# Moving Softplus behind the visit's Square and cutting the Erfs of the second group in two halves

## The chip, the cores and the metric

The kernel runs on one core of one Trainium2 chip (trn2). The metric is the device time of one execution in microseconds (us). A core has five engines that work side by side, each through its own list of instructions in order: TensorE (PE in the profile, with its weight loads as PEld), VectorE (DVE), ScalarE (ACT), GpSimd (POOL) and SyncE (SP), which starts the DMA transfers.

## What is computed

An attention block without softmax, its output normalised by its root mean square, and behind it a feed-forward block with the gate h * erf(softplus(h)).

```python
# q, k, v: (8, 8, 576, 64)   g_norm: (64,)
kv = np.einsum('bhsd,bhse->bhde', k, v)
out = np.einsum('bhsd,bhde->bhse', q, kv)
rms = np.sqrt(np.mean(out * out, axis=-1, keepdims=True) + 1e-06)
x = out / rms * g_norm                 # then (B, H, S, D) -> (B*S, H*D) = (4608, 512)
# w_in: (512, 2048)   w_out: (2048, 512)
h = x @ w_in
sp = np.maximum(h, 0.0) + np.log1p(np.exp(-np.abs(h)))
g = h * erf(sp)
y = g @ w_out                          # (4608, 512)
```

## The kernel before

**Groups and units.** The 4608 rows are worked on in nine groups of 512 rows. A group T < 8 holds the first 512 rows of one batch element; the ninth holds the last 64 rows of all eight. The hidden width 2048 is cut into FC = 16 units of 128, and BATCH = 4 units make a period. For one unit, TensorE makes a 128 x 512 block of h; ScalarE and VectorE bring it to SBUF and gate it; TensorE multiplies it with w_out.

**Two stages.** In the first stage (the loop over n from L848, groups T = 0 and 1, here called group 1 and group 2) the weights are also converted and cut. Group 1 uses plain fp32 products (L900). Group 2 multiplies with cut forms: every product (`product`, L651) makes two partial results, n_ps with 8 matmuls and m_ps with 4 (L659). ScalarE copies n_ps to h with a scale (L915), VectorE adds m_ps (L637), ScalarE takes the Softplus (L928), and after each fourth unit the Erfs (L935); VectorE multiplies h by the result (`gates`, L846) LAG - 1 = 4 units later, and one unit after that the plain projection with w_out runs (L715). In group 2 ScalarE also starts the cut of weights for the later groups (`w_upper`, L621), which VectorE finishes (L624, L627) and the SP queue stores to DRAM.

In the second stage (the loop over m from L1001, groups T = 2 to 8) both products use cut forms that are loaded back from DRAM (`load_parts`, L799). A period has four hidden products, each with a copy of n_ps (L1050), an add of m_ps (L637) and a Softplus (L1065); then two Erfs over half of the period's columns each (L1071, or the second of them at L1094); then four products with w_out for the period before (`result`).

**Visits.** Between these stands the attention for the next group, in four visits for each group, one for two heads, and cut into pieces that are put at places of the period. For T = 3 to 7 of the attention (it runs while the feed-forward works on T - 1) the pieces are: loads; the visit itself (matmuls L460 to L474, the Square L479, VectorE's halving of it L505 and L506, and L482, L366, L373, which keep what the next visit needs); a transpose of q (L343); the mean (matmuls L521 and L522, then Ln, Exp and Square, L536 to L538); the norm (L544 to L556); the split into cut forms (ScalarE's upper part L597, VectorE's lower parts L600 and L603). The visit stands at place 2, behind unit 1. The mean stands at place 5, behind the first result, and in a group's last period (`last_`) at place 4, ahead of it.

**Order and buffers.** The order is written out by hand: each engine gets its instructions in the order in which the program issues them, under a manual schedule. `pieces(place)` issues all pieces that are due at a place. ScalarE's functions come from table sets, of which one is loaded at a time: Softplus, Erf, and Ln with Exp stand in different sets; `softplus_table()` (L109) and `exp_ln_table()` (L106) load theirs ahead of use, and the Erf set is loaded in front of the first Erf. In the first stage n_ps and m_ps have one pair of PSUM banks (`turns=False`), so that the next unit's n_ps needs the copy of the last; in the second stage three pairs take turns. The mean's matmuls write columns of the visit's PSUM tile that hold the tail and the next kv product until L482 and L366 have read them.

Of the kernel before, what the change touches and what calls it, by code (L numbers as in the profile page):

```python
# [43 lines left out]
AF = mybir.ActivationFunctionType  # L44
# [6 lines left out]
BATCH = 4  # L51
# [3 lines left out]
FIRST = 2  # L55
# [6 lines left out]
def kernel(  # L62
# [10 lines left out]
    nc = tc.nc  # L73
# [8 lines left out]
    FC = DF // P  # L82
# [25 lines left out]
    def softplus_table():  # L108
        nc.scalar.preload_act_table_set("softplus")  # L109
# [195 lines left out]
    def weights():  # L305

        w_next("split")
        w_next("join")
        w_next("load")
# [77 lines left out]
    def keep_prepared():  # L387
        kept.pop()()
        turn(1, 0)
# [230 lines left out]
    def upper_w(x, high):  # L620
        nc.scalar.activation(high, x, AF.Copy, scale=(1.0 + 2.0**-13) / SHIFT)  # L621
# [48 lines left out]
    def w_upper(which, f, place=None):  # L670


        if place is None:
            t = w_in_p.tile([P, 3, G], FP32R, name="w_new", tag="w")
            parts = t.rearrange("p i (c f) -> p i c f", c=KC)
        else:
            t = None
            parts = w_in_sb.bitcast(FP32R)[:, 3 * place : 3 * (place + 1)]
        if which == "in":
            x = w_in_sb[:, f]  # L680
        else:
            x = w_out_sb[:, f, :].rearrange("p (c f) -> p c f", c=KC)
        upper_w(x, parts[:, 0])
        w_new[which, f] = t, x, parts
# [100 lines left out]
    first_batch, batches = FIRST * NB, NG * NB  # L785
# [50 lines left out]
    hs, ss, plain = {}, {}, {}  # L836
    whole = FIRST * FC - BATCH

    def due(k):

        i = w_at["join"] + k
        ahead = 1 if LAG - 2 <= n < LAG + BATCH else 2
        return i < len(w_order) and w_order[i][0] <= n + ahead

    def gates(n):
        nc.vector.tensor_tensor(out=hs[n], in0=hs[n], in1=ss[n], op=ALU.mult)  # L846

    for n in range(FIRST * FC + 1):  # L848
        T, f = divmod(n, FC)
        if n == FC:  # L850
            early_room.close()
            late = ctx.enter_context(tc.tile_pool(name="late", bufs=1))
            x_new = ctx.enter_context(tc.tile_pool(name="x_new", bufs=1))
            acc = ctx.enter_context(tc.tile_pool(name="acc", bufs=1))
            w_in_p = ctx.enter_context(tc.tile_pool(name="w_in_p", bufs=BATCH))
            low = low_room.enter_context(tc.tile_pool(name="low", bufs=1))
            forms = late.tile([P, 3, KC, G], FP32R, name="x_forms0")
            x_forms[FIRST] = [forms[:, i] for i in range(3)]
        if T < FIRST:
            if f == 0:  # L860
                steps = pieces_of(T + 1)

            if due(0 if n == 2 * (BATCH - 1) else 1):
                weights()
            while kept:
                keep_prepared()
            for piece in steps[f][3]:
                piece()
            for key in list(w_new)[:2]:
                w_lower(*key)  # L870
            for piece in steps[f][0]:
                piece()
        while due(0):
            weights()
        done = n - LAG + 1
        if T == 0 and done >= 0:
            gates(done)
        if T == FIRST - 1:
            if f == 0:
                x_high = wide.tile([P, KC, G], FP32R, name="x_high", tag="a")  # L880
                x_low = low.tile([P, KC, G], FP32R, name="x_low")
                for i in range(0, KC, 2):
                    upper(xT[T][:, i : i + 2], x_high[:, i : i + 2])
                for i in range(0, KC, 2):
                    lower_only(xT[T][:, i : i + 2], x_high[:, i : i + 2], x_low[:, i : i + 2])
        if T == FIRST - 1 and f >= WHOLE:
            n_ps, m_ps = hidden(T, f, turns=False)
        elif T < FIRST:

            if n > 1:  # L890
                plain[n] = ps_h.tile([P, G], FP32, name="h_ps", tag="h")
                blocks = [(n, c) for c in range(KC)]
            elif n == 0:
                for i, (pool, tag) in enumerate(((ps_at, "at"), (ps_o, "o0"))):
                    plain[i] = pool.tile([P, G], FP32, name="h_ps", tag=tag)
                blocks = [(i, c) for c in range(KC - 1) for i in range(2)] + [(0, KC - 1)]
            else:
                blocks = [(1, KC - 1)]
            for i, c in blocks:
                nc.tensor.matmul(  # L900
                    plain[i],
                    lhsT=w_in_sb[:, i % FC, c],
                    rhs=xT[T][:, c, :],
                    start=(c == 0),
                    stop=(c == KC - 1),
                )
        if T < FIRST:
            if n == whole:
                old_h = acc.tile([P, BATCH, G], FP32, name="h", tag="e")
            h = hs[n] = old_h[:, n - whole] if n >= whole else unit("h_sb")  # L910
            s = ss[n] = unit("s_sb")
            if n in plain:
                nc.scalar.copy(h, plain.pop(n))
            else:
                nc.scalar.activation(h, n_ps, AF.Copy, scale=SHIFT - 1.0)  # L915
                add(h, m_ps)
            if T == FIRST - 1:
                if f == 1:
                    x_both = wide.tile([P, KC, G], FP32R, name="x_both", tag="b")
                    for i in range(0, KC, 2):  # L920
                        both_only(x_high[:, i : i + 2], x_low[:, i : i + 2], x_both[:, i : i + 2])
                    x_forms[T] = x_high, x_low, x_both
                gates(done)
                for key in list(w_new):
                    w_lower(*key)
                for key in to_cut[f]:
                    w_upper(*key)
            nc.scalar.activation(s, h, AF.Softplus)  # L928
            if n == 0:
                w_next("split")  # L930
            for piece in steps[f][1]:
                piece()
            if f % BATCH == BATCH - 1:
                for i in range(n - BATCH + 1, n + 1):
                    nc.scalar.activation(ss[i], ss[i], AF.Erf)  # L935
                softplus_table()
            if T == FIRST - 1:
                load_parts("in", {FC - 3: 2, FC - 2: 1, FC - 1: 1}.get(f, 0))
        if n >= LAG:
            T2, f2 = divmod(n - LAG, FC)  # L940
            last = n - LAG in (FC - 1, whole - 1)
            project(f2, hs[n - LAG], last)
            if last:
                sums(*((acc, "e") if T2 < FIRST - 1 else (wide, "a")))
                if T2 == 0:
                    for j in range(J):
                        store(T2, j, es.pop(j))
        if T < FIRST:
            for piece in steps[f][2]:
                piece()  # L950
            fetch_some(4)
# [49 lines left out]
    for m in range(first_batch, batches + 1):  # L1001
        T, b = divmod(m, NB)
# [23 lines left out]
        def pieces(place):  # L1026
            while todo and places[-len(todo)] <= place:
                todo.pop(0)()
# [10 lines left out]
        if m < batches:  # L1039

            pool, tag = (acc, "e") if m % 2 else (wide, "b")
            h = pool.tile([P, BATCH, G], FP32, name="h", tag=tag)
            s = gate_r.tile([P, BATCH, G], FP32, name="s", tag="s")
        for i in range(BATCH):
            if m < batches:
                n_ps, m_ps = hidden(T, b * BATCH + i)
            fetch(i)

            def evacuate():
                nc.scalar.activation(h[:, i], n_ps, AF.Copy, scale=SHIFT - 1.0)  # L1050
                add(h[:, i], m_ps)


            early_copy = i == 0 and b == 0 and first_batch < m < batches
            if early_copy:
                evacuate()
            if i == 0:
                for half in range(done, 2):
                    g.append(cut_upper(old_h, half))
            if i == 0 and not done:  # L1060
                cut_lower(old_h, 0, g[0])
            if m < batches:
                if not early_copy:
                    evacuate()
                nc.scalar.activation(s[:, i], h[:, i], AF.Softplus)  # L1065
            if i == BATCH - 1:
                cut_lower(old_h, 1, g[1])
            pieces(i + 1)
        if m < batches:
            for i in range(1 if last_ else 2):  # L1070
                nc.scalar.activation(part(s, i), part(s, i), AF.Erf)  # L1071
            if len(todo) < 2:
                softplus_table()
# [63 lines left out]
```

## Time and profile before

| | us |
|---|---|
| median of 3 runs | 918.5 (918.29 to 918.88) |
| the profiled execution, whole | 917.64 |
| its span in the profile | 915.9 |
| one product in the second stage, n_ps and m_ps (start to start) | 2.72 |
| one period with a visit (start of L460 to the next), mostly | 23.81 |

The costliest groups that the change bears on, from the page's part 5. The columns are: line, engine, operation, output and input with their shapes, count | busy us, mean ns of one | idle us of the engine before them, and what ended most of it.

```profile
L1065 ACT ACTIVATE s<-h 128x512 f32<-128x512 f32 x112 | 70.9, 633 | 181.0 <-DVE h L637 181.0
L637 DVE TENSOR_TENSOR h<-m_ps,h 128x512 f32<-128x512 f32 x116 | 79.8, 688 | 61.4 <-ACT h L1050 40.3
L1050 ACT ACTIVATE h<-n_ps 128x512 f32<-128x512 f32 x112 | 65.4, 584 | 14.6 <-PE n_ps L659 14.6
L109 ACT ACT_TABLE_LOAD x44 | 56.5, 1283 | 0.7
```

Here ScalarE is idle for 181 us in front of Softpluses, each of which waits for VectorE's add; VectorE is idle for 61 us in front of these adds, mostly for ScalarE's copies. Idle time of an engine that isn't the bound costs nothing by itself. In timelines a line is: start in us, duration, engine, source line, operation, output and input, count, and in brackets the idle time of the engine before it with what ended that. A matmul's end is modelled, so durations of neighbours overlap, and distances are best read from start to start.

### The profile page before, as it was taken

What the parts mean: (1) busy time and instruction counts of PE and PEld (TensorE: products, weight loads), DVE (VectorE), ACT (ScalarE), POOL (GpSimd) and SP (SyncE); (2) the same over time, 40 slices, a digit from 0 to 9 for tenths busy, and PEclk for the clock granted to TensorE, in tenths of its full rate; (3) what the DMA queues carried; (4) which work ended last, traced back from release to release, by engine and by line L of the source; (5) the groups of instructions that cost most, each with busy time, mean ns of one, the idle gap of its engine ahead of it and who ended that gap; (6) DMA issues with size and microseconds to landing.
All of it is one profiled execution on the core that took longest, in us unless ns stands there. A gap on an engine that the chain in (4) does not pass through costs nothing.

```text
span 915.9 us, 13573 instructions
## 1 busy us (share of the span) xinstructions
PE 896.3 (98%) x4990; PEld 668.1 (73%) x4990; DVE 750.1 (82%) x1088; ACT 589.2 (64%) x783; POOL 2.4 (0%) x10
## 2 busy tenths in 40 slices
PE   6999999999999999999999999999999999999998
PEld 4444445656678888887888788878888788888886
DVE  2889958898588888888888888888888888887777
ACT  3877666776766666666666666666666766665552
POOL 1000000000000000000000000000000000000000
PEclk9999999999999999999999999999999999999999
DMA  9877507889799998999799988999796687778771
GB/s 264 249 233 223 156 1 262 332 330 349 233 345 371 347 318 262 344 345 314 233 337 336 328 277 292 344 330 307 266 361 265 253 307 312 289 285 327 315 263 48
DMA packets 145954, 259.91 MB, mean 284 GB/s; under 512 B 82016, under 2 KB 104544, under 8 KB 145888
## 3 DMA queue, kind: packets, MB, share of 16 engines
q1 hardware_dynamic: 144176, 256.75, 82.1%
q10 hardware_dynamic: 1648, 2.29, 0.8%
q8 instruction: 40, 0.66, 0.3%
q14 instruction: 26, 0.21, 0.1%
q0 software_dynamic: 64, 0.00, 0.0%
HBM read 224.40 MB, written 34.60 MB: 283 GB/s over the span
## 4 chain that ended last, share of the span: by engine, by line
PE 72%; DVE 10%; DMA 8%; ACT 6%; issue 2%; SPq 1%; DVEq 0%; ACTq 0%
PE n_ps L659 38%; PE m_ps L659 19%; PE h_ps L900 6%; PE o_ps L715 5%; DMA q_sb<-in_q_dram 3%; DVE e L637 1%; PE at_ps L474 1%; PE at_ps L460 1%; DMA w_out_parts<-w_out 1%; DVE h L1097 1%; DVE h L637 1%; DVE e L632 1%; ACT s_sb L935 1%; DMA q_last<-in_q_dram 1%; DMA out_dram<-e 1%
## 5 line engine op out<-in xcount | busy, mean ns | idle before, releaser
L659 PE MATMUL n_ps<-w_out_parts,g_forms 128*128 128x512 f32 x928 | 230.5, 390 | 0.3 <-DMA w_out_parts<-w_out 0.3
L659 PE MATMUL n_ps<-x_forms,w_in_parts 128*128 128x512 f32 x896 | 224.4, 392 | 0.0
L659 PEld LDWEIGHTS n_ps<-w_out_parts,g_forms 128*128 128x128 f32 x928 | 172.7, 188 | 36.1 <-DMA w_out_parts<-w_out 0.7
L659 PEld LDWEIGHTS n_ps<-x_forms,w_in_parts 128*128 128x128 f32 x896 | 166.6, 188 | 35.6 <-issue 0.2
L1065 ACT ACTIVATE s<-h 128x512 f32<-128x512 f32 x112 | 70.9, 633 | 181.0 <-DVE h L637 181.0
L637 DVE TENSOR_TENSOR h<-m_ps,h 128x512 f32<-128x512 f32 x116 | 79.8, 688 | 61.4 <-ACT h L1050 40.3
L659 PE MATMUL m_ps<-w_out_parts,g_forms 128*128 128x512 f32 (+1 forms) x468 | 124.2, 388 | 0.0
L659 PE MATMUL m_ps<-x_forms,w_in_parts 128*128 128x512 f32 x448 | 119.7, 389 | 0.0
L715 PE MATMUL o_ps<-w_out_sb,h_sb 128*128 128x512 f32 x224 | 101.5, 596 | 0.2 <-DVE h_sb L846 0.2
L659 PEld LDWEIGHTS m_ps<-w_out_parts,g_forms 128*128 128x128 f32 x468 | 87.4, 188 | 18.4
L659 PEld LDWEIGHTS m_ps<-x_forms,w_in_parts 128*128 128x128 f32 x448 | 84.1, 188 | 17.5
L637 DVE TENSOR_TENSOR e<-m_ps,e 128x512 f32<-128x512 f32 (+1 forms) x117 | 80.3, 687 | 13.9 <-PE m_ps L659 2.0
L1050 ACT ACTIVATE h<-n_ps 128x512 f32<-128x512 f32 x112 | 65.4, 584 | 14.6 <-PE n_ps L659 14.6
L715 PEld LDWEIGHTS o_ps<-w_out_sb,h_sb 128*128 128x128 f32 x224 | 41.3, 189 | 45.2 <-issue 42.9
L603 DVE SCALAR_TENSOR_TENSOR g_forms<-g_forms 128x1024 fp32r<-128x1024 f32 x58 | 71.1, 1225 | 2.0
L600 DVE TENSOR_TENSOR g_forms<-h,g_forms 128x1024 fp32r<-128x1024 f32 x58 | 70.6, 1217 | 1.2 <-ACT g_forms L597 1.1
L597 ACT ACTIVATE g_forms<-h 128x1024 fp32r<-128x1024 f32 x58 | 59.0, 1051 | 16.8 <-PE m_ps L659 11.1
L1097 DVE TENSOR_TENSOR h<-h,s 128x1024 f32<-128x1024 f32 x56 | 65.9, 1217 | 0.0
L900 PE MATMUL h_ps<-xT,w_in_sb 128*128 128x512 f32 x144 | 64.6, 594 | 0.2 <-DVE w_in_sb L288 0.2
L632 DVE SCALAR_TENSOR_TENSOR e<-n_ps,e 128x512 f32<-128x512 f32 x88 | 60.1, 682 | 1.0 <-PE n_ps L659 0.9
L109 ACT ACT_TABLE_LOAD x44 | 56.5, 1283 | 0.7
L900 PEld LDWEIGHTS h_ps<-xT,w_in_sb 128*128 128x128 f32 x144 | 27.1, 190 | 33.7 <-issue 31.3
(119 smaller groups left out, 987.8 us busy)
## 6 DMA issues: line engine op xcount, KB each, us to landing
w_out_parts<-w_out SPq DMA_DIRECT2D x116, 768.0 KB, 7.3
w_in_parts<-w_in SPq DMA_DIRECT2D x112, 768.0 KB, 6.9
w_in<-w_new SPq DMA_DIRECT2D x16, 768.0 KB, 4.7
w_raw<-in_moe_w_in_dram SPq DMA_DIRECT2D x16, 512.0 KB, 5.0
w_raw<-in_moe_w_out_dram SPq DMA_DIRECT2D x8, 1024.0 KB, 5.5
out_dram<-e SPq DMA_DIRECT2D x32, 256.0 KB, 4.2
k_sb<-in_k_dram SPq DMA_DIRECT2D x28, 280.0 KB, 7.4
v_sb<-in_v_dram SPq DMA_DIRECT2D x28, 280.0 KB, 7.6
```

Source lines behind the costliest of these rows:

```text
L109: nc.scalar.preload_act_table_set("softplus")
L597: nc.scalar.activation(high, x, AF.Copy, scale=1.0 + 2.0**-13)
L600: nc.vector.tensor_tensor(out=low, in0=x, in1=high.bitcast(FP32), op=ALU.subtract)
L603: nc.vector.scalar_tensor_tensor(out=both, in0=low.bitcast(FP32), scalar=SHIFT, in1=high.bitcast(FP32), op0=ALU.mult, op1=ALU.add,)
L632: nc.vector.scalar_tensor_tensor(out=out_, in0=ps, scalar=scale, in1=out_, op0=ALU.mult, op1=ALU.add)
L637: nc.vector.tensor_tensor(out=out_, in0=ps, in1=out_, op=ALU.add)
L659: nc.tensor.matmul(ps[:, cols], lhsT=weights(form, k), rhs=moving(form, k)[:, cols], start=(form == forms[0] and k == 0), stop=(form == fo ...
L715: nc.tensor.matmul(o_ps[j], lhsT=g[:, j * P : j * P + P], rhs=w_out_sb[:, f, :], start=(f == 0), stop=last,)
L900: nc.tensor.matmul(plain[i], lhsT=w_in_sb[:, i % FC, c], rhs=xT[T][:, c, :], start=(c == 0), stop=(c == KC - 1),)
L1050: nc.scalar.activation(h[:, i], n_ps, AF.Copy, scale=SHIFT - 1.0)
L1065: nc.scalar.activation(s[:, i], h[:, i], AF.Softplus)
L1097: nc.vector.tensor_tensor(out=part(h, half), in0=part(h, half), in1=part(s, half), op=ALU.mult)
```

## The change

In group 2 (T = FIRST - 1 = 1) the four Erfs after units 3, 7 and 11 are cut in two. Two of them stay where they were, without the softplus table behind them. The other two, and the table load, are issued in the next unit, behind its copy of h, its add and its weight cuts, and ahead of its Softplus. After unit 15 all four Erfs stay together.

In the second stage the Softpluses of a period's units 0 and 1 are no longer issued behind their own copies, but both together after the pieces of place 2. In a period with a visit that is behind the visit's Square. Units 2 and 3 keep theirs.

```diff
+    def erf(units):
+        for i in units:
+            nc.scalar.activation(ss[i], ss[i], AF.Erf)
+
     for n in range(FIRST * FC + 1):
...
+            if T == FIRST - 1 and f and f % BATCH == 0:
+                erf(range(n - BATCH // 2, n))
+                softplus_table()
             nc.scalar.activation(s, h, AF.Softplus)
             if n == 0:
                 w_next("split")
             for piece in steps[f][1]:
                 piece()
             if f % BATCH == BATCH - 1:
-                for i in range(n - BATCH + 1, n + 1):
-                    nc.scalar.activation(ss[i], ss[i], AF.Erf)
-                softplus_table()
+                apart = T == FIRST - 1 and f < FC - 1
+                erf(range(n - BATCH + 1, n + 1 - (BATCH // 2 if apart else 0)))
+                if not apart:
+                    softplus_table()
...
+            def softplus(i):
+                nc.scalar.activation(s[:, i], h[:, i], AF.Softplus)
+
             early_copy = i == 0 and b == 0 and first_batch < m < batches
...
             if m < batches:
                 if not early_copy:
                     evacuate()
-                nc.scalar.activation(s[:, i], h[:, i], AF.Softplus)
+                if i > 1:
+                    softplus(i)
             if i == BATCH - 1:
                 cut_lower(old_h, 1, g[1])
             pieces(i + 1)
+            if m < batches and i == 1:
+                softplus(0)
+                softplus(1)
```

Set side by side, the lists of the two programs differ on ScalarE alone. Around a visit that list is, before and after (h a copy of n_ps, s a Softplus, sq the Square):

```
before   h0  s0  h1  s1  sq  h2  s2  h3  s3
after    h0  h1  sq  s0  s1  h2  s2  h3  s3
```

## The prediction

> **What bounds the kernel now.** I read the page first, for the engines and the releasers, then the list of waits, then the timelines of TensorE, ScalarE (ACT) and VectorE (DVE) around every place where TensorE loses its rhythm.
>
> ```profile
> PE 896.3 (98%) x4990; PEld 668.1 (73%) x4990; DVE 750.1 (82%) x1088; ACT 589.2 (64%) x783; POOL 2.4 (0%) x10
> ...
> PE 72%; DVE 10%; DMA 8%; ACT 6%; issue 2%; SPq 1%; DVEq 0%; ACTq 0%
> ```
>
> TensorE is the bound. The other engines count only where they make it late, so the question is which of its delays the change removes. The list of waits has the candidates (waiting engine and line, releaser, us in total, times, longest):
>
> ```profile
> DVE h L637 <- ACT h L1050: 40.3, 45, 1.2
> DVE sq_hi L505 <- ACT sq L479: 23.7, 20, 1.2
> PE at_ps L521 <- DVE bd_kv L366: 2.1, 3, 0.9
> PE n_ps L659 <- ACT h_sb L915: 0.9, 1, 0.9
> PE at_ps L521 <- DVE x_last L482: 0.9, 1, 0.9
> ```
>
> The first two are long, but they are VectorE's own idle time. The last three are TensorE's. They seem to be only 3.9 us, but a wait that ends inside the pipeline is shown short, so I measured each from the spacing of starts.
>
> Group 2 first, at the boundary after a period's fourth unit. TensorE's timeline, then ScalarE's:
>
> ```profile
> 187.83 3.60 PE L715 MATMUL o_ps<-w_out_sb,h_sb 128*128 128x512 f32 x8
> 192.36 0.49 PE L659 MATMUL n_ps<-x_high,w_new 128*128 128x512 f32 x1 [0.93 <-ACT h_sb L915]
> 192.69 0.39 PE L659 MATMUL n_ps<-x_low,w_new 128*128 128x512 f32 x1
> ```
>
> ```profile
> 186.41 1.28 ACT L935 ACT_TABLE_LOAD   x1
> 187.70 2.19 ACT L935 ACTIVATE s_sb<-s_sb 128x512 f32<-128x512 f32 x4
> 189.90 1.28 ACT L109 ACT_TABLE_LOAD   x1
> 191.20 0.63 ACT L597 ACTIVATE x_forms<-x 128x512 fp32r<-128x512 f32 x1
> 191.73 0.58 ACT L915 ACTIVATE h_sb<-n_ps 128x512 f32<-128x512 f32 x1
> ```
>
> The copy of h (L915), which frees the one n_ps bank of this group, stands behind a table load, four Erfs and another table load. From the first o_ps start to the second matmul of the next n_ps TensorE takes 4.86 us here; at an undisturbed unit (181.59 to 185.26) it is 3.67. Lost: 1.19. The same reading at the next boundary (215.90 to 219.91) gives 4.01, lost 0.34; at the first (160.96 to 164.62) 3.66, nothing.
>
> Then the last visit of a group in the main loop, at 417 to 426 us. TensorE, ScalarE, VectorE:
>
> ```profile
> 425.06 0.36 PE L521 MATMUL at_ps<-sq_hi,mean_w 128*128 128x256 f32 x1 [0.92 <-DVE bd_kv L366]
> ```
>
> ```profile
> 420.40 0.63 ACT L1065 ACTIVATE s<-h 128x512 f32<-128x512 f32 x1 [4.09 <-DVE h L637]
> 420.94 0.58 ACT L1050 ACTIVATE h<-n_ps 128x512 f32<-128x512 f32 x1
> 422.28 0.63 ACT L1065 ACTIVATE s<-h 128x512 f32<-128x512 f32 x1 [0.76 <-DVE h L637]
> 422.81 0.58 ACT L479 ACTIVATE sq<-at_ps 128x512 f32<-128x512 f32 x1
> ```
>
> ```profile
> 419.68 0.68 DVE L637 TENSOR_TENSOR h<-m_ps,h 128x512 f32<-128x512 f32 x1
> 421.55 0.69 DVE L637 TENSOR_TENSOR h<-m_ps,h 128x512 f32<-128x512 f32 x1 [1.19 <-ACT h L1050]
> 423.43 0.43 DVE L505 CAST sq_hi<-sq 128x512 fp32r<-128x512 f32 x1 [1.18 <-ACT sq L479]
> ```
>
> A ping-pong: the first Softplus waits for VectorE's first add, the second copy stands behind that Softplus, VectorE waits 1.19 for the copy, then the same again over the Square (1.18). The mean's matmuls write columns that L366 still has to read, and are held. Where the mean follows the visit directly, consecutive n_ps starts are 3.19 us apart undisturbed (2.72 for a product and 0.47 for the mean). At the five last visits of T = 2 to 6 they are 3.34, 4.33, 3.99, 3.99 and 4.31. Lost: 0.15 + 1.14 + 0.80 + 0.80 + 1.12 = 4.01. At the other visits the mean stands one product later and the spacing is 3.19.
>
> **The Trainium skill.** "ScalarE: Activation LUTs", section "What ACT_TABLE_LOAD costs", gives about 1283 ns for a load and 1380 ns for a drain. The trace has 1.28 us, but the next instruction starts 0.01 us later: no drain; I use 1.28. The same page, "Table sets: the hidden batching unit", says that cheap functions such as copy are in every set. So the copies that now stand between two halves of the Erfs need no load of their own; in the trace copies do run under the softplus table (L915 after L109). "Perfetto Trace Analysis", section "Matmuls", advises rotating PSUM banks so that one evacuation overlaps the next product. The trace agrees: the single pair of group 2 is caught by a late copy, the three pairs of the main loop are not.
>
> **The change part by part.** It touches only ScalarE's order: instructions on the other four engines, their order and the count of table loads stay the same.
>
> *Erf in halves, three boundaries.* Before L915 go two Erfs (2.19/2 = 1.10 us) and one table load (1.28): the copy comes 2.38 us earlier, or when its product is ready. At 192.36 it then ends near 189.9, and TensorE wants the bank near 191.2: 1.3 us to spare; the whole 1.19 goes, and at the next boundary the 0.34. The two Erfs and the load go behind the copy and the cuts of weights (L621), ahead of the next Softplus (L928). What is queued behind them is that Softplus and the next copy. Nothing there becomes later: the total up to that point is equal, and part of it fills the 0.56 us that the Softplus waited for VectorE at 164.82. The gates that read the second half of the Erfs are VectorE's two units later. x_forms (L597) is also 2.38 us earlier, which takes up to 1.55 to 2.88 us of VectorE's idle time. That matters, since VectorE is busy for 25 us of each 27 to 28 here and would otherwise be the next limit. Estimated gain 1.53, bounds 0 and 1.8 (the 0.23 us that TensorE waits at 240.70 for a gate hangs on a mean, an Exp and a norm that all shift with TensorE: I leave it).
>
> What is late next is the first w_out load of the main loop. TensorE waits 0.25 us for it at 258.45; it was issued at 246.75, when the last gates (L846) released its space. Those gates wait for Erfs and e copies that follow TensorE's last projections, so the load shifts by the same 1.53. From 250 to 340 us the DMA share is 1.03 or more, so a load that did not shift would cost TensorE the gain. I take nothing off and keep 1.5 for the range.
>
> *Softplus behind the Square, 28 periods, 20 of them with a visit.* Removed from between the copies are two Softpluses (0.53 us each, back to back) and, above all, their two waits. At 417 to 426: the second copy can run at about 417, when its product is done; the second add follows the first at 420.29 in place of 421.55; the Square is done by 419.1; the cast starts at about 420.9 in place of 423.43, 2.5 us earlier. L366 ends near 422.4. TensorE reaches the mean at 425.06 - 0.92 = 424.14, so all five losses go, with 1.7 us to spare: 4.01.
>
> Behind the Square now wait both Softpluses, the third copy and its add. The Square waits for the visit's matmuls (L460, from 417.12), so the first Softplus still runs at about 420.4, when its add is done; the third copy runs near 421.6, before 423.29. In the eight periods without a visit nothing stands between the second copy and the Softpluses, and the spacing there is already TensorE's: zero.
>
> What is late next is the following group's x_forms. Their lower part (L600) ends at 436.16, 0.34 us before TensorE starts on it at 436.50. The chain to it (add, Softplus, copy, Softplus, Ln, Exp, norm, upper, lower) hangs on L366 and moves by the 2.5 us; TensorE wants 1.14: enough. Were the chain not to follow, 0.8 of each larger gain would be lost. Elsewhere the 2.3 us that VectorE gains in each visit end as waiting for TensorE: zero.
>
> **Sum.** 1.53 + 4.01 = 5.54 us. The profiled execution has a span of 915.9 and took 917.64 (1.74 around it): span about 910.4, execution 912.1. The median of the runs shown is 918.5, 0.86 above that execution: 918.5 - 5.5 = 913.0.
>
> **Rivals.**
> - *The loads don't shift* (for: DMA share 1.03 at 250 to 260; against: VectorE's release at 246.75 and a quiet queue before). The Erf half is worth nothing: 918.5 - 4.0 = 914.5.
> - *The wait only moves to x_forms* (for: 0.34 us of slack; against: it hangs on the same Square). Each of the four larger gains shrinks to 0.34, with the 0.15 together 1.5 of the 4.01: 918.5 - 1.5 - 1.5 = 915.5.
> - *TensorE is paced by itself*, the gaps return as equal ones elsewhere: 918.5.
> - *Slower: weight cuts hold the Erfs.* L621 waits for stores to free its buffers (0.48 and 1.22 us at 175 to 177), the DMA share is 0.97 from 167 to 195, and the second Erf half and its load, 2.38 us, stand behind the cuts now. If the cuts at a boundary wait more than the 4.6 us by which the next copy is early (it ends at 167.06, TensorE wants the bank at 171.7), each of three boundaries costs up to 2.38 and the 1.53 isn't earned: 918.5 + 7.1 - 4.0 = 921.6. Against: what those buffers held was handed to the stores over 7 us before, and the median landings here are 3.4 to 5.2.
>
> **How the numbers follow.** Forecast 0.77; loads don't shift 0.09; x_forms 0.05; no change 0.05; slower 0.04. What a measurement of this kernel can tell from no change is 0.2%, 1.84 us. The first three are faster by more: 0.91; same 0.05; slower 0.04. The forecast's own range is 911.8 (with the 0.23 and 0.25 waits gone too, and some transitions) to 914; the two weaker gains take it to 915.2.
>
> **What would show it.** Right: no wait of L521 on L366 or L482; n_ps spacing 3.19 at all means; 3.67 at the boundaries of group 2; L505's wait on L479 nearly gone; the span of group 2 (140.44 to 249.82) shorter by 1.5. Wrong: a PE wait on w_out_parts of over 1 us near 257, one on x_forms at a group's start, or an unchanged L521.

## The result and the profile after

The median is 912.37 us (911.94 to 913.5 in 4 runs) against 918.39 us for the kernel before beside it (917.6 to 918.88): a ratio of 0.9937, with an interval of 0.992 to 0.9954. The forecast was 913.0. The profiled execution took 912.39 us, its span is 910.6. Some lines have other numbers in the changed kernel: the copies L915 and L1050 are L919 and L1058, the Softpluses L928 and L1065 are L935 and L1063, the Erfs L935 are L850.

The page's part 4, the chain of work that ended last (share of the span by engine), is now TensorE almost alone, where it had 72% before:

```profile
PE 93%; DMA 3%; ACT 2%; DVE 1%; issue 0%; SPq 0%; DVEq 0%; ACTq 0%
```

The list of waits (engine and line, releaser, us in total, times, longest). Some of its lines, most of them in answer to those of before:

```profile
ACT h L1058 <- PE n_ps L659: 74.1, 80, 3.3
ACT s L1063 <- DVE h L637: 70.1, 64, 1.7
DVE h L637 <- PE m_ps L659: 67.6, 57, 3.9
...
DVE sq_hi L505 <- ACT sq L479: 1.9, 4, 0.5
DVE h L637 <- ACT h L1058: 1.4, 2, 1.2
...
PE n_ps L659 <- DMA w_out_parts<-w_out: 0.8, 1, 0.8
```

VectorE hardly waits for ScalarE's copies and Squares any more (1.4 and 1.9 us, 40.3 and 23.7 before), but for TensorE's products. ScalarE still waits for VectorE's adds, 70.1 us where it was 181.0, and longer than before for products. TensorE's waits on L366, L482 and the copy are gone from the list. Of the waits behind group 2 one stays there, for a w_out load, 0.8 us where it was 0.3; those ahead of group 2, mostly for loads, are as before.

The boundary of group 2, ScalarE's timeline, then TensorE's:

```profile
184.20 1.28 ACT L850 ACT_TABLE_LOAD   x1
185.49 1.16 ACT L850 ACTIVATE s_sb<-s_sb 128x512 f32<-128x512 f32 x2
186.56 0.61 ACT L597 ACTIVATE x_forms<-x 128x512 fp32r<-128x512 f32 x1
187.07 0.58 ACT L919 ACTIVATE h_sb<-n_ps 128x512 f32<-128x512 f32 x1
...
189.11 1.14 ACT L850 ACTIVATE s_sb<-s_sb 128x512 f32<-128x512 f32 x2
190.26 1.28 ACT L109 ACT_TABLE_LOAD   x1
191.56 0.63 ACT L935 ACTIVATE s_sb<-h_sb 128x512 f32<-128x512 f32 x1
```

```profile
187.44 3.60 PE L715 MATMUL o_ps<-w_out_sb,h_sb 128*128 128x512 f32 x8
190.47 0.79 PE L659 MATMUL n_ps<-x_high,w_new 128*128 128x512 f32 x1
191.10 0.39 PE L659 MATMUL n_ps<-x_low,w_new 128*128 128x512 f32 x1
```

From the start of o_ps to the second matmul of n_ps it is 3.66 us, the undisturbed figure, where it was 4.86. The copy ends at 187.65, 2.8 us before TensorE starts on the bank at 190.47.

The last visit at 414 to 423 us: ScalarE, VectorE, TensorE.

```profile
414.82 0.60 ACT L1058 ACTIVATE h<-n_ps 128x512 f32<-128x512 f32 x1 [1.86 <-PE n_ps L659]
417.06 0.60 ACT L479 ACTIVATE sq<-at_ps 128x512 f32<-128x512 f32 x1 [1.64 <-DVE h L637]
417.55 1.14 ACT L1063 ACTIVATE s<-h 128x512 f32<-128x512 f32 x2
```

```profile
416.34 1.28 DVE L637 TENSOR_TENSOR h<-m_ps,h 128x512 f32<-128x512 f32 x2
417.69 0.43 DVE L505 CAST sq_hi<-sq 128x512 fp32r<-128x512 f32 x1
...
418.89 0.28 DVE L366 TENSOR_REDUCE bd_kv<-at_ps 128x64 f32<-128x128 f32 x1
```

```profile
419.76 1.98 PE L659 MATMUL n_ps<-x_forms,w_in_parts 128*128 128x512 f32 x8
...
422.48 0.28 PE L521 MATMUL at_ps<-sq_hi,mean_w 128*128 128x256 f32 x1
...
422.95 0.40 PE L659 MATMUL n_ps<-w_out_parts,g_forms 128*128 128x512 f32 x1
```

The two adds now stand in one line, since nothing comes between them, and the cast follows with no wait in brackets. L366 is done at 419.2, 3.3 us before the mean. From the n_ps ahead of the mean (419.76) to the one behind it (422.95) it is 3.19 us, and so it is at all five of these visits. The one mean in the second stage that is still held is that of the first period, at 258.6 (4.30 us), behind the wait for the w_out load.

To see where the time came from I cut every trace at the starts of L460, the first matmuls of a visit. "Group 2" runs from its first visit to the first visit of the second stage, "first period" from there to the next visit, "main" from there to the last visit, "tail" from there to the end of the span.

| us | up to group 2's first visit | group 2 | first period | main | tail | span |
|---|---|---|---|---|---|---|
| before | 140.44 | 109.38 | 24.35 | 431.30 | 210.4 | 915.9 |
| after | 140.04 | 107.82 | 24.92 | 428.51 | 209.3 | 910.6 |
| difference | -0.40 | -1.56 | +0.57 | -2.79 | -1.1 | -5.3 |

The first column holds nothing that the change touches; over all runs of this study it lies between 140.04 and 141.24. The first period holds the wait for the w_out loads. The others repeat to 0.15 us from run to run, except group 2 with its old order and the tail of one kernel below, so they decide what the whole time, which scatters by more than 1 us, can't.

### The profile page after: what moved, and what is told of

Its sections match the earlier page's. It is cut to its first block, busy times and chain, and to the rows that moved or that the text cites. A ratio compares the mean times of both kernels' runs of the same rounds, so it can differ in the third digit from the quotient of the medians.

```text
span 910.6 us, 13577 instructions
## 1 busy us (share of the span) xinstructions
PE 894.7 (98%) x4990; PEld 668.8 (73%) x4990; DVE 750.4 (82%) x1088; ACT 592.1 (65%) x783; POOL 2.4 (0%) x10
## 4 chain that ended last, share of the span: by engine, by line
PE 93%; DMA 3%; ACT 2%; DVE 1%; issue 0%; SPq 0%; DVEq 0%; ACTq 0%
PE n_ps L659 48%; PE m_ps L659 24%; PE o_ps L715 10%; PE h_ps L904 6%; PE at_ps L474 2%; PE at_ps L460 2%; DMA w_out_parts<-w_out 1%; DMA v_sb<-in_v_dram 1%; PE at_ps L521 1%; PE at_ps L522 1%; DMA q_last<-in_q_dram 1%; ACT rms_r L536 0%; PE ms_ps L527 0%; ACT rms_r L537 0%; DVE h L846 0%
## 5 line engine op out<-in xcount | busy, mean ns | idle before, releaser
L1058 ACT ACTIVATE h<-n_ps 128x512 f32<-128x512 f32 x112 | 66.2, 594 | 74.3 <-PE n_ps L659 74.1
L1063 ACT ACTIVATE s<-h 128x512 f32<-128x512 f32 x112 | 68.3, 629 | 70.1 <-DVE h L637 70.1
```

## The experiments

Each kernel ran in five rounds beside the kernel before, the first one in 21. The first four undo or narrow one half of the change.

**The Erf half alone.** The Softpluses are put back:

```diff
-                if i > 1:
-                    softplus(i)
+                softplus(i)
...
-            if m < batches and i == 1:
-                softplus(0)
-                softplus(1)
```

> The Erf half of the change alone; every Softplus of the main loop stands as before. Theory: the losses at the boundaries of group 2 (1.19 and 0.34 us) go, so that the stretch from its first to its last visit (140.44 to 249.82 before) is 1.5 us shorter, and about 0.6 comes back as a longer wait for the first w_out loads: 1.0 us net, ratio 0.999; the five means keep their spacings of 3.34, 4.33, 3.99, 3.99, 4.31. Rival (TensorE paced by itself): the stretch stays at 109.4 us. Rival (loads arrive just the same): 1.5 us net.

Measured: 916.92 us, before 918.3; ratio 0.9982 (0.9976 to 0.9989). Group 2 is 107.84, the first period 24.64, main 431.33, tail 210.4. So this half is worth 1.54 us in its own stretch; the first period is 0.3 us longer. The medians differ by 1.38 us, and the interval (1.0 to 2.2 us) holds both the 1.0 that was expected and the 1.5 of the second rival, so it doesn't decide between them. The five spacings stay (3.25, 4.32, 3.95, 4.01 and 4.30), and with them the wait at the last visits, as TensorE's timeline shows:

```profile
424.11 0.35 PE L521 MATMUL at_ps<-sq_hi,mean_w 128*128 128x256 f32 x1 [0.89 <-DVE bd_kv L366]
```

**The Softplus half alone.** The Erfs are put back together:

```diff
-            if T == FIRST - 1 and f and f % BATCH == 0:
-                erf(range(n - BATCH // 2, n))
-                softplus_table()
...
-                apart = T == FIRST - 1 and f < FC - 1
+                apart = False
```

> The Softplus half alone; group 2 keeps its four Erfs together. Theory: all five means at 3.19 us, 4.0 us less than before, ratio 0.9956; the boundaries of group 2 keep 4.86 and 4.01. Rival (the two halves need each other, since the wait only moves to the next x_forms): under 2 us, with a wait of TensorE at the groups' starts.

Measured: 914.51, before 918.3; ratio 0.9959 (0.9946 to 0.9971). Main is 428.52 and the tail 209.3, the changed kernel's numbers; together 3.8 us less. There is no wait at the groups' starts, so the halves don't need each other. In group 2 (109.84) the copy is late again, and the boundary takes 5.36 us, 0.5 more than before. The old order varies there: the four profiles that have it give 109.35, 109.38, 109.40 and 109.84 for group 2.

```profile
192.58 0.49 PE L659 MATMUL n_ps<-x_high,w_new 128*128 128x512 f32 x1 [1.43 <-ACT h_sb L919]
```

**The Softplus half in the groups' last periods alone.** As above, and:

```diff
-                if i > 1:
+                if i > 1 or not last_:
                     softplus(i)
...
-            if m < batches and i == 1:
+            if m < batches and i == 1 and last_:
```

> The Softplus half, but only in each group's last period (6 of 28); no Erf half. Theory: the other periods' gain is VectorE's idle time alone, so this gives the same 4.0 us as the whole Softplus half, within 0.5. Rival (VectorE's lead adds up over a group's periods): clearly less than the Softplus half, by over 1 us, with spacings of the means between 3.19 and those of before.

Measured: 914.21, before 918.3; ratio 0.9958 (0.9944 to 0.9971). Main 428.52, tail 209.3: the whole gain, from 6 of 28 periods. VectorE still waits 17.8 us for Squares in the others, and that costs nothing. What the rival named does happen: at a last visit VectorE's first add starts 1.59 us behind L460 here, and 0.73 with the whole Softplus half. But it is reserve, not time.

**Behind the second copy, but ahead of the Square.** As in the second experiment, and:

```diff
-            pieces(i + 1)
             if m < batches and i == 1:
                 softplus(0)
                 softplus(1)
+            pieces(i + 1)
```

> No Erf half; the first two Softpluses behind the second copy, but ahead of the visit's pieces, so ahead of the Square. Theory: the first turn of the ping-pong is gone (the second add follows the first), the second stays shorter; the cast L505 starts about 1.3 us earlier than before where 1.14 is lost at most, so the means come down to 3.19 to 3.3 and the time is 3.5 to 4.0 us less than before. Rival (the Square's place is what counts): half of the loss stays, about 2 us less than before, spacings of the large means near 3.6.

Measured: 914.95, before 918.3; ratio 0.9961 (0.9949 to 0.9974). Main 428.52, tail 209.3: the whole gain again. Its VectorE timeline at a last visit shows that the second turn of the ping-pong is still there:

```profile
418.97 1.28 DVE L637 TENSOR_TENSOR h<-m_ps,h 128x512 f32<-128x512 f32 x2
421.43 0.43 DVE L505 CAST sq_hi<-sq 128x512 fp32r<-128x512 f32 x1 [1.18 <-ACT sq L479]
```

VectorE waits those 1.18 us at all 20 visits, 23.7 us as before, and TensorE doesn't notice. What paid was that the second copy no longer stands behind the first Softplus; the place behind the Square adds reserve. At the visit shown it is 2.2 us from the end of L366 to the mean, in the third experiment 2.6 and in the second 3.3.

The next ones start from the whole change and try its neighbours.

**The mean behind the first result in the last periods.**

```diff
-            places = (0, 0 if T + 1 == B else 2, 2 if T + 1 == B else 3, 4, 5, 5, 6)
+            places = (0, 0 if T + 1 == B else 2, 2 if T + 1 == B else 3, 5, 5, 5, 6)
```

> The whole change, and in a group's last period the mean stands behind the first result (place 5 in place of 4), so that it comes 2.72 us later on TensorE, and ScalarE has one table load more between its halves. Theory (the next group's x_forms are what is late next): ScalarE's Ln then waits for a table load, an Erf and a table load, so x_forms comes some 2.3 us later, where it is 2.2 us early in the changed kernel (431.66 against 433.89 at the first group boundary after 400): a wait of up to 0.9 us at each of six group starts, 0.5 to 5 us slower than the changed kernel. Rival (TensorE has reserve in its order, the chain is not tight): the same time as the changed kernel within 0.5 us.

Measured: 913.11, before 918.14; ratio 0.9947 (0.9934 to 0.9959). Main 428.52, tail 209.6. Main, with four of the six group starts, didn't change, as the rival has it. VectorE's and TensorE's timelines at the group start at which x_forms comes latest:

```profile
719.24 0.68 DVE L600 TENSOR_TENSOR x_forms<-x,x_forms 128x512 fp32r<-128x512 f32 x1
```

```profile
719.42 1.98 PE L659 MATMUL n_ps<-x_forms,w_in_parts 128*128 128x512 f32 x8
```

The lower part ends at 719.92. TensorE starts the group at 719.42 and its second matmul at 719.65, and doesn't wait. In the kernel a visit writes only its own quarter of x_forms (index p, in `split_lower`), and `product` takes the quarters in order, the upper and the lower part of each. So the last visit's lower part is first read by the eighth matmul, which starts at 721.01, 1.1 us after it is ready; at four of the other starts it is ready 1.44 us ahead, at the last one 1.38. I had counted from the first matmul. The chain to x_forms came about as much later as expected (2.4 us at the start at 434), and TensorE had more reserve than that: 3.8 us in the changed kernel. Only the tail is longer, by about 0.3; its two group starts show no wait either, but two products in the period behind the first of them stand 2.83 and 2.88 us from the ones before in place of 2.72. What holds them is open.

**k and v ahead of the w_out loads.** The DMA queues are idle while the loads wait for the last gates:

```diff
+    load_pair((FIRST + 1) * NP + 2, later=True)
+    fetch_some(4)
     load_parts("out", BATCH)
...
+            if m == first_batch:
+                todo[0] = lambda: None
```

> The whole change, and the k and v loads of the first visit of the second stage are issued ahead of the first four w_out loads, into the 5 us in which the DMA is idle (240 to 244.8), and no longer behind them. Theory (the fourth w_out load, 10.9 us in flight, is slowed by the 0.6 MB of k and v beside it): it lands 1 us or more earlier, the 0.82 us wait of TensorE at 257 goes, 0.3 to 0.8 us less than the changed kernel, first period 24.1 us in place of 24.9. Rival (the landing is set by the loads themselves or by chance): the first period stays between 24.3 and 24.9.

Measured: 912.38, before 918.14; ratio 0.9938 (0.9926 to 0.9951). The first period is 23.96. TensorE's timeline there, of the changed kernel and then of this one:

```profile
254.72 1.52 PE L659 MATMUL n_ps<-w_out_parts,g_forms 128*128 128x512 f32 x6
257.06 0.73 PE L659 MATMUL n_ps<-w_out_parts,g_forms 128*128 128x512 f32 x2 [0.82 <-DMA w_out_parts<-w_out]
```

```profile
255.32 2.17 PE L659 MATMUL n_ps<-w_out_parts,g_forms 128*128 128x512 f32 x8
```

The fourth load was 10.0 us in flight in place of 10.9. It is still not alone: two q loads now stand right behind the w_out loads (issued at 247.60), where k and v stood. The kernel was run once more beside the changed kernel:

> The changed kernel once more, beside the next two on one chip. Theory: group 2 at 107.8 us, the periods from the second to the last visit at 428.5, the tail at 209.3 as in its first profile; the first period of the second stage, which holds the wait for the w_out loads, is the one stretch that varies from run to run, anywhere between 24.3 and 24.9. Rival (the longer wait there belongs to the change): 24.9 again.

> k and v ahead of the w_out loads, once more, beside the changed kernel. Theory: the first period at 24.0 us again and the median 0.3 to 0.9 us below that of the changed kernel beside it. Rival (chance): the first period above 24.3, no difference of medians.

The changed kernel: 912.99 (ratio 0.9938, 0.9925 to 0.995), first period 24.71. With k and v ahead: 912.65 (0.9932, 0.9919 to 0.9946), first period 24.50, with a wait of 0.4 us. The second expectation named 24.0, and that didn't come back. The two stretches are lower than the changed kernel's two, but by 0.2 to 1.0 us, and the single runs overlap (911.5 to 912.82 against 912.32 to 913.36): whether it helps is not settled.

**All four Erfs behind the next copy.**

```diff
-                erf(range(n - BATCH // 2, n))
+                erf(range(n - BATCH, n))
                 softplus_table()
...
-                erf(range(n - BATCH + 1, n + 1 - (BATCH // 2 if apart else 0)))
                 if not apart:
+                    erf(range(n - BATCH + 1, n + 1))
                     softplus_table()
```

> The whole change, but all four Erfs stand behind the next copy of h, none ahead. Theory: the copy comes early enough already with two, so nothing more is gained; VectorE's gate of the first unit, which stands right behind the add, now waits about 1 us for its Erf, and VectorE has some 2 us of idle time in each such period: the same time as the changed kernel within 0.7 us. Rival (VectorE is the next limit in group 2): its waits come back as waits of TensorE for m_ps, 1 to 3 us slower, group 2 (140 to 248) longer by as much.

In this kernel the gate of a period's first unit is issued ahead of its Erf, so for three units it multiplies by the Softplus alone. I had missed that, and with it the wait that I expected on VectorE: the wait is ScalarE's, for the gate to have read. ScalarE's timeline:

```profile
189.92 1.28 ACT L850 ACT_TABLE_LOAD   x1
192.70 2.19 ACT L850 ACTIVATE s_sb<-s_sb 128x512 f32<-128x512 f32 x4 [1.49 <-DVE h_sb L846]
```

Measured: 913.34, before 918.14; ratio 0.9948 (0.9935 to 0.9962); group 2 is 107.86. So even this order, which leaves the Erf out of three gates, is no faster than the changed kernel's. And it shows why not all four can go behind the copy: the first Erf can't be moved that far without the gate moving too. A form with the gate behind its Erf wasn't tried.

**Only the table load behind the copy**, all four Erfs ahead of it:

```diff
-                erf(range(n - BATCH // 2, n))
                 softplus_table()
...
-                erf(range(n - BATCH + 1, n + 1 - (BATCH // 2 if apart else 0)))
+                erf(range(n - BATCH + 1, n + 1 - 0))
```

> The whole change, but all four Erfs stay ahead of the copy and only the load of the softplus table goes behind it. Theory: the copy comes 1.28 us earlier than before, the largest loss there was 1.19, so the boundaries are free too and the time is that of the changed kernel within 0.5 us; cutting the Erfs in halves only adds reserve. Rival (the Erfs ahead of the copy are what delays it): a loss of 0.3 us or more stays at the boundary near 190.

Measured: 912.91, before 918.14; ratio 0.9947 (0.9934 to 0.9959). Group 2 is 107.84: the whole of the Erf half's gain, from moving one load of 1.28 us.

```profile
188.65 0.61 ACT L597 ACTIVATE x_forms<-x 128x512 fp32r<-128x512 f32 x1
189.17 0.57 ACT L919 ACTIVATE h_sb<-n_ps 128x512 f32<-128x512 f32 x1
```

The copy ends at 189.74 here, and TensorE starts on the bank at 191.11, unhindered. That is a reserve of 1.4 us, where the whole change has 2.8.

**The parts that pay, together**: the table load alone behind the copy, the Softpluses moved in last periods only and ahead of the pieces, and k and v ahead.

> What the earlier runs leave of the change, with k and v ahead: the softplus table's load alone goes behind the copy in group 2 (all four Erfs stay together ahead of it), and the first two Softpluses go behind the second copy, ahead of the pieces, in a group's last period alone. Theory: these are the parts that pay, so all four stretches are those of the run with k and v ahead and the whole change (108.0, 24.0, 428.5, 209.4) and the time is the same within 0.6 us. Rival (the rest of the change adds reserve that is needed once the parts meet): 0.6 us or more slower, and a wait of TensorE for a copy or for L366 comes back.

Measured: 912.45 (912.25 to 912.5), before 918.63; ratio 0.9932 (0.992 to 0.9945). The stretches are 107.84, 24.51, 428.52 and 209.3. The first period is the one that misses its 24.0; it is that of the second run with k and v ahead. No wait of TensorE for a copy or for L366 came back, though the reserve at the last visits is down to 1.3 us (0.9 at the last of them). The rest of the change isn't needed for the time; nor does this version beat the changed kernel beyond the scatter of the runs.

## Why the prediction was right, step by step

- *The sum.* 5.54 us were forecast; the spans differ by 5.3 and the medians beside each other by 6.0 (interval 4.2 to 7.3). That the spans come so close is in part luck: 0.40 us ahead of group 2, which the change doesn't touch, nearly make up for the 0.57 that the first period lost. The stretches that the forecast named give 1.56 + 3.9.
- *Erf in halves: 1.53.* Measured 1.56 in the whole change and 1.54 alone. The reserve was under-rated, 1.3 us where it is 2.8: I had the copy ending near 189.9, it ended at 187.65, which is 188.05 counted from the same start of group 2. Only the instructions directly ahead of it were counted; VectorE's idle time for x_forms had gone too, and the Softplus ahead of the Erfs, which waits for VectorE's add, came sooner (183.55 in place of 185.76, 0.40 of it the earlier start). Nothing turned on it: the table load alone would have done.
- *Softplus behind the Square: 4.01.* Measured 2.79 + 1.1 = 3.9, all of it from the last visits; the kernel before made up for the other 0.15 within the same periods. That the last read of the columns holds the mean can be told from the kernel before: counted from L460, this read (L366, at the last of the five L482) ends at 6.80, 7.79, 7.45, 7.45 and 7.20 us, and each of the five losses is that time less 6.65 (6.08 at the last, where the mean follows L460 0.56 us sooner). The first of the two waits alone would have done: with the Softpluses behind the second copy, but ahead of the Square, the gain is the same. The reserve was under-rated here too, 1.7 us where it is 3.3. At the visit shown the cast starts 2.07 us behind the start of L460 (415.62) in place of 6.31 (417.12), so 4.2 us earlier where 2.5 were forecast: 2.4 of it lie between the first add and the cast, and 1.8 are that VectorE comes to the first add sooner.
- *The w_out loads shift with group 2.* They did: issued at 244.81 in place of 246.75, as group 2's end demands. The wait still grew from 0.25 to 0.82. It isn't given back by the Erf half: with the old Erfs the first period is 24.35, 24.34, 24.53 and 24.82, with the new ones and the old place of k and v 24.92, 24.71, 24.64, 24.71, 24.64 and 24.71. The ranges overlap; the means are 24.51 and 24.72. A part of some 0.2 us may belong to the change; the rest goes with the flight of the fourth load, 10.3 to 10.9 us, which reaches 10.9 with the old Erfs as well (fourth experiment). Counted by starts this wait costs 1.1 us near 257 (4.30 in place of 3.19), the size that I had named as a sign of being wrong, but by the same count it was 0.55 before. My rival, in which the loads don't shift, is out; that the same loads could simply take longer was not among the cases.
- *x_forms is what is late next.* It moved along, as forecast, but it was not tight. The 0.34 us of slack were counted from the group's first matmul; the eighth, the first that reads the last visit's lower part, starts at 438.08, 1.9 us after the 436.16 at which that part ends. So there was less to fear than I said, and the rival, which took the 0.34 for all there was, had the same error. It falls with the second experiment, where the whole gain is there without a wait.
- *VectorE's gain at the other visits is worth zero, and nothing needs the two Softpluses early.* Shown by the third and fourth experiments.
- *Slower through weight cuts that hold the Erfs.* No sign of it: the cuts at 187.55, 188.07 and 188.59 follow the copy without a wait, and no cut of group 2 waits for a store in this profile.

## What to carry to other kernels

Where an engine's list mixes an instruction that frees a buffer with one that only has to be done some time, put the freeing one first, and ask of each waiting instruction who is queued behind it: one copy behind one Softplus was two engines' ping-pong. Measure the bound engine's losses by distances of starts, at each place by itself, since a wait listed as 0.9 us was 1.1 to 1.2; here their sum was what the change could bring at these places. And once the loss is gone, more reserve brings nothing: 6 of 28 periods and one table load out of an edit in many places held all of the gain. To tell how much reserve a place has, count from the instruction that reads the piece that comes last, not from the first of its product: at x_forms that was 1.9 us in place of 0.34.

## What was not expected

The stretches in which TensorE is the only limit repeat to 0.01 us (main is 428.51 to 428.53 in all eleven profiles of kernels with these Softpluses moved). Nearly all of the scatter between these profiles lies in two places: the time up to group 2, which spans 1.2 us, and the wait for the first w_out loads, from none listed to 0.8 us. In the first of them TensorE waits 7.0 to 8.5 us for v's loads, but these waits don't follow the differences from run to run, so its cause is open.
